# W1 staged in W2's tile and in the second `hT` buffer, with a new order of all operations

## The chip, the cores and the metric

The kernel runs on one core of one Trainium2 chip. The metric is the device time of one launch in microseconds; the time before is the median of three runs.

The core has five engines that run their own instruction streams: TensorE (PE in the profile; its weight loads are PEld), VectorE (DVE), ScalarE (ACT), GpSimd (POOL) and SyncE (SP), which here only issues DMAs. Loads of the first batch, of v and of W1 are issued by SP, casting loads (fp32 in memory, fp16 on chip) by POOL.

## The reference

Nystrom attention with 32 landmarks, in fp32, over 8 batches, 8 heads, 576 positions and 64 columns per head. Then, on the heads put side by side (`x` is 8 x 576 x 512), a normalisation, two products with a relu between them, and the residual.

```python
q_lm = q.reshape(B, H, 32, 18, D).mean(axis=3)
k_lm = k.reshape(B, H, 32, 18, D).mean(axis=3)
A, Bm, C = sm(q, k_lm), sm(q_lm, k_lm), sm(q_lm, k)     # softmax of scaled products
Z = Bm^T / (norm1(Bm) * norminf(Bm) + 1e-06)
for _ in range(6):
    Z = 2 * Z - Z @ Bm @ Z
x = heads_side_by_side(A @ Z @ C @ v)                   # 8 x 576 x 512
xn = (x - mean) / sqrt(var + 1e-06) * g_ln
out = x + maximum(xn @ w_ch1, 0) @ w_ch2                # 512 -> 2048 -> 512
```

## The kernel before

**Operations and their order.** Every piece of work is a named operation with the buffers that it uses and the engines that may do it. `op(name, engines, uses, fn)` only records it. At the end one loop goes through the list `ORDER`, 1571 entries of an operation's number and an engine's letter (P, D, A, G, S for PE, DVE, ACT, POOL, SP), and emits them. So that list sets the order of instructions on each engine, and which engine does what. A buffer takes a slot of its kind at its first use and gives it back behind its last use, so the list also decides who shares a slot with whom: kind `stg` has 6 slots (staged fp32 inputs), `p2` and `bank` are the PSUM kinds (2 and 4 slots), `nat` has 3, and `hT0` and `hT1` one each.

**Batch 0**, the first some 25 us, has a path of its own. SP loads its k, q and v as fp32 into `stg` slots, two units of four heads each (operations `load_k00`, `load_k01` and so on). They are cast to fp16, transposed by PE (`pst_k`, `pst_q`), summed to landmarks by PE (`pss_k`, `pss_q`), and copied out as `klm` and `qbd`. From these come the 32 x 32 softmax, six iteration steps (PE into `it`, DVE into `st`), the exponentials `ea` and `ect`, their normalisation through `psd` and `lns`, `product_0` (`pscv`, with v), `zt` and `zcbd`.

**The second half of each batch.** `psy` (operation `rows`) makes blocks of 128 rows of `x` from `ea` and `zcbd`. `psm` multiplies `zt` by a quarter of W1, and DVE or ACT makes `m` of it. For batches 0 and 1, `m` also takes up `less`, W1's column means, which PE makes in `psf` and ACT copies out, so that the mean of `x` is taken off. `psh` makes one of 16 hidden chunks (128 hidden columns, 576 positions) in one of the two `p2` slots. A relu on ACT (L203) or DVE (L1068) takes it into `hT`. `pso` multiplies `hT` by W2; batches 2 to 7 do that with seven products instead of eight for most blocks (`ps7a`, `ps7c`, `ps7e`), with sums (`mix`) made by POOL and DVE. The last block of all is cut into part a (384 columns) and part b (128 columns), each with its products, its closing addition on DVE (L210, `x<-pso_74a` and `x<-pso_74b`) and its stores.

**The weights.** `def_weights` loads W1 in 8 pieces of 128 x 2 x 512 fp32 by SP (`load_w1_0` to `load_w1_7`; piece i is half of hidden quarter i/2), each into a `stg` slot (`w1s`). 16 scalings multiply each half piece by g into the fp16 tile `w1_16` (two a piece, on POOL, DVE or ACT, which `ORDER` says). Four casting loads on POOL's queue bring W2 into `w2_16`. A W1 piece can only be loaded when one of the six `stg` slots is free, and these hold k, q and v of batch 0 first.

**Fillers.** `warm_0` is 24 idle matmuls of 160 columns into a `bank` slot; `warm_1` to `warm_14` are 4 idle matmuls of 128 columns each. They compute nothing that is used.

**Batch 1 and later** come from POOL's casting loads, `load_q10` the first of them, into `nat` slots, and are transposed by DVE (`xT_q<-nat_q`). Batch 1's landmark sums are made by PE (`psl`) and copied out as `tot`.

In the rows of the instruction lists below, `w_16_78` is W1's fp16 tile, `w_16_79` is W2's, `natv_76` and `natv_77` are v of batches 0 and 1, `w1s` a staged piece of W1.

Of the kernel before, what the change touches and what calls it, by code (L numbers as in the profile page):

```python
# [24 lines left out]
145P 169D 104A 168D 98S 254D 149P 150D 147P 148A 172P 173A 176P 247P 177A 248A 259D 255D 174P 175A
246D 256P 257A 146A 170P 171D 109G 110G 121P 122P 123P 111G 124P 268P 156P 258D 151D 249D 267P 112A
125A 275A 269A 270A 271A 157D 277A 158D 131P 132P 133P 134P 178P 163P 278D 279D 117G 273A 433G 274A
99S 113G 135A 180D 263S 164A 159P 280P 281D 160A 165P 166A 114G 264A 100S 115G 116G 265S 118G 136P
137P 266G 161P 179D 429G 119G 138P 139P 162D 282P 283D 140A 181P 182A 183P 284P 276D 285A 143P 187P
184D 286P 144A 188A 272D 152D 185P 186A 287D 297P 298D 299D 189P 191D 190D 288P 289A 294P 290P 295A  # L30
201P 202P 296A 300P 301A 291D 292P 293A 120G 455G 212P 213P 435G 436G 437G 310P 438G 445G 302A 303G
308P 309A 214P 330P 434D 444D 312D 311D 313D 332D 192P 193A 153D 154D 198P 199A 155A 441D 430D 439D
431D 331D 442D 440D 432D 443D 234P 556D 215P 304P 235P 236P 305A 306A 196P 446G 447G 203P 204P 194P
195A 237P 238P 205P 206P 451G 197A 307G 314P 315A 337P 339P 448G 449D 822G 338A 555D 239P 240P 241P
322P 207P 208P 574D 565D 569G 450D 340A 323A 216P 242D 209D 210S 217P 324D 341P 343D 223P 335P 244S
336A 342D 333P 463D 218P 219P 577G 452D 220D 344P 352P 353D 467G 468G 469G 470G 334A 826G 348P 345A
349A 346P 347A 457G 318P 319A 224P 316P 317A 225P 226P 227P 481P 458G 465D 459G 460G 482A 350P 454D
354D 357P 471D 464D 472D 351A 453D 363P 228P 229P 364D 358A 361P 230P 362A 461D 462D 365D 493P 494A
359P 368P 360A 483P 495P 355P 325D 326D 505A 369A 356A 231D 233A 200G 374P 375P 366P 367A 370P 371A
573G 506D 456D 507P 508P 509D 320P 321D 385P 484P 486A 487A 489A 510P 834D 511D 466D 491A 386P 387P  # L40
485A 388P 211S 512P 376P 473S 474G 490A 377P 496P 498A 501A 499A 497A 513D 514P 327D 488D 492D 328D
396P 397P 475S 476G 566G 828G 829G 830G 831G 572G 477S 478G 838G 839G 844G 564G 568G 503A 378P 379P
380P 515D 823D 502A 221S 504D 372P 516P 479S 480A 500D 517D 836D 528P 529P 530D 531D 398P 399P 373A
381P 522P 518P 389P 329A 866S 382D 418P 519D 824D 559D 520P 521D 523A 532P 419P 420P 524A 533A 534A
558D 550P 551D 552D 553D 548P 549A 421P 422P 423P 536P 424P 425P 848G 535G 832D 833D 554D 232S 867A
537A 538A 539G 560D 525P 527A 400P 401P 557D 426D 427S 605P 526A 606A 840G 841G 594P 595A 561D 540P
541A 390P 391P 611P 612A 837D 596D 827D 392P 393D 825D 850G 851G 852G 563D 603P 604A 853G 562D 859D
842D 860G 861G 843D 579P 613P 614A 407P 580A 601P 602A 609P 610A 1217G 585P 408P 845D 599P 409P 607P
600A 410P 411P 586A 597P 608A 542A 543G 856D 615P 598A 576G 626P 616A 412P 413P 581P 627A 402P 862G
394S 582A 570G 567D 617D 589D 835D 863G 858D 590D 618P 619A 634P 635A 643P 583P 584A 620P 621A 624P  # L50
414P 571G 874P 625A 622P 623A 628P 629A 644P 544P 847D 857D 545A 846D 591D 546A 875D 403P 632P 872S
633A 645P 630P 647P 592D 631A 646P 415D 877P 648P 649P 650P 864D 865D 854D 404D 855D 1191G 886P 638D
637G 641G 663P 664P 665P 639D 640D 662G 428S 417S 406S 661D 593A 882A 884A 879A 880A 883A 652D 878A
651D 657D 887A 889P 892A 896A 658D 666P 668D 894A 895A 849D 667D 653P 654P 711P 722P 712A 723A 891A
890A 655P 656P 547G 575G 675P 676P 677P 728P 729A 678P 695P 696A 1192D 713D 716P 881D 1194D 717A
724P 725A 876P 888P 1213G 660D 587P 870S 714P 416S 659D 871G 873G 384S 1229G 642G 1230G 1231G 726P
898A 715A 679D 682D 669P 897D 727A 588A 730P 222S 1232G 899D 900P 901P 731A 718P 732P 902D 743P 719D
578G 903P 904D 670P 720P 734A 733A 721D 744A 671P 672P 673D 699P 700A 893D 739P 636G 1203D 1239S
701P 905P 243S 741P 906D 740A 751P 674D 742A 703P 752A 907P 735P 736A 737P 383S 868S 681S 680S 683S
738A 702D 908D 909P 1219G 1195G 1220G 1221G 685P 704D 697P 698A 915P 917A 916A 910D 911P 1222G 759P  # L60
760P 749P 811P 925P 750A 761P 885D 869G 921P 926A 927A 753G 922P 1225D 755G 912D 913P 705D 706D 745P
746A 1227D 812P 707D 708D 709D 710A 813P 814P 747P 748A 686P 687P 688P 928G 929P 930A 1223D 1224D
1196D 1233D 815P 816P 923D 1228D 924D 914D 931A 1214D 943P 947D 944D 941P 817P 946D 945D 1240G 754G
# [12 lines left out]
1026D 1027D 1254D 1279D 1266D 1011G 1022P 1297G 1070P 1023P 1024P 1025P 1029D 1028D 1005G 1068P
1069D 1286A 1298P 1290P 1299A 1291P 1292D 1010D 1293D 1280P 1281D 1091P 1032P 1033P 1038P 1300A
1301G 1092A 1287P 1071D 1289A 1288A 1282P 1283D 1039P 1040P 1312P 1314D 1313D 1316D 1315D 1080P
1082A 796S 1099P 1100A 1081A 1034P 1035P 806S 1310P 1311A 1097P 1036D 1098A 1041P 1306P 1101P 1307A
1095P 1096A 1037D 1030D 1044P 1043D 1093P 1094A 1089P 1090A 1042D 1074D 1075D 1031G 807S 1045P 1046P  # L80
1083P 1084D 1047P 1103A 1051D 1317P 1318A 1087P 1088A 1102D 1085P 1086A 1054P 1052S 1055P 1106P
1107A 1104P 1048D 1049S 1105D 1319P 1320A 1056P 1057P 1061D 1076D 1108P 1058D 1109A 1110P 1111A
1122G 1126G 1124G 1180P 1181P 1112P 1113A 1063S 1343P 1332P 1344A 1182P 1183P 1114P 1115A 1128P
1129P 1120P 1121D 1118P 1119A 1130P 1131P 1053S 1116P 1117A 1077D 1078D 1351P 1352D 1079A 1308A
1309G 1123G 1125G 1137D 1062S 1136D 1184P 1185P 1349P 1350A 1186P 1187P 1302P 1138P 1334D 1333A
1337P 1303A 1132P 1133P 1338D 1188D 1134P 1347P 1348D 1341P 1342D 1135P 1143D 1142D 1148P 1050S
1190S 1327D 1149P 1150P 1304A 1323P 1151P 1153D 1324D 1152D 1345P 1346A 1339P 1340A 1139P 1140P
1141P 1335P 1353P 1147D 1144D 1145D 1354A 1364P 1336D 1355D 1146D 1127G 1154P 1155P 1365A 1325P
1326D 1156P 1189A 1360P 1361A 1356P 1357A 1157P 1370P 1160P 1161P 1372P 1305D 1433P 1162P 1435P
# [19 lines left out]
def kernel(  # L109
# [112 lines left out]
    def dma(e, o, i):  # L222
        keep(ENGINES[e].dma_start(out=o, in_=i))
# [1040 lines left out]
```

## Time and profile before

| | |
|---|---|
| time, median of 3 runs | 260.66 us (260.17 to 260.79) |
| span of the profiled execution | 258.5 us |
| PE busy | 249.9 us (97%) |
| PE weight loads | 179.8 us (70%) |
| DVE busy | 212.3 us (82%) |
| POOL busy | 177.5 us (69%) |
| ACT busy | 163.9 us (63%) |
| DMA, SP's queue | 23.37 MB, 29.6% of 16 engines' span |
| DMA, POOL's queue | 10.36 MB, 25.1% |
| granted TensorE clock | 0.9 or more in each of 40 slices |

One execution was profiled, and its own time is the span in the table, 258.5 us, from the first instruction to the last; the timed median lies 2.2 us above it. In the rows of the profile, L and a number is a line of the kernel before; `a<-b` says that a is written from b; sizes are partitions x columns. A row of the timeline begins with the start in us from the span's beginning and a duration, of one instruction or of a row of alike ones up to the end of the last; what stands in brackets is the idle time before it and who ended it. `SP` issues, `DMA` rows are transfers.

Read by slices, PE is busy nearly throughout, and its first slice is at seven tenths. The DMA engines move 234 to 374 GB/s in the first five of the 40 slices.

### The profile page before, as it was taken

How to read it: one execution, taken by the hardware profiler on the slowest of the kernel's cores; microseconds unless marked ns; L12 is line 12 of the kernel's file. 1: busy time of each engine (PE TensorE's matmuls, PEld its weight loads, DVE VectorE, ACT ScalarE, POOL GpSimd, SP SyncE). 2: the span in 40 equal slices, each digit the busy share in tenths (PEclk: the TensorE clock that was granted, in tenths of full speed). 3: DMA queues.
4: the chain of work that ended last, by engine and by line, in shares of the span. 5: the costliest groups of instructions: out<-in, count | busy, mean ns of one | idle time of the engine just before them, and what ended most of it. 6: DMA issues, size and time to landing. Idle time of an engine off the chain costs nothing.

```text
span 258.5 us, 8351 instructions
## 1 busy us (share of the span) xinstructions
PE 249.9 (97%) x3499; PEld 179.8 (70%) x3499; DVE 212.3 (82%) x472; ACT 163.9 (63%) x304; POOL 177.5 (69%) x180
## 2 busy tenths in 40 slices
PE   7898999999999999999999999999999999999993
PEld 7766465556554557777766787777867787788981
DVE  1669899999999989997998869898547999878661
ACT  1588886747766999778756997868666245644000
POOL 8324899689794789699999995782078505966600
PEclk9999999999999999999999999999999999999999
DMA  6999999999749176949704832500130100510356
GB/s 234 367 269 338 374 210 208 207 235 244 227 127 178 29 164 87 221 89 286 140 4 121 231 93 61 127 3 3 41 85 0 44 20 9 115 23 20 82 121 184
DMA packets 23277, 36.32 MB, mean 140 GB/s; under 512 B 2116, under 2 KB 11592, under 8 KB 23240
## 3 DMA queue, kind: packets, MB, share of 16 engines
q1 hardware_dynamic: 12456, 23.37, 29.6%
q0 software_dynamic: 9504, 10.36, 25.1%
q10 hardware_dynamic: 1280, 2.07, 3.1%
q8 instruction: 27, 0.44, 0.7%
q14 instruction: 10, 0.08, 0.1%
HBM read 36.70 MB, written 9.44 MB: 178 GB/s over the span
## 4 chain that ended last, share of the span: by engine, by line
PE 85%; DMA 7%; ACT 3%; DVE 2%; issue 1%; SPq 1%; ACTq 0%; DVEq 0%
PE psh L193 23%; PE ps7a L193 16%; PE pso L193 15%; PE ps7c L193 8%; DMA w1s<-in_moe_w_ch_dram 5%; PE ps7e L193 4%; PE psm L193 3%; PE psy L193 3%; DMA stg_q<-in_q_dram 3%; PE it L193 2%; PE pscv L193 2%; PE psd L193 1%; PE psec L193 1%; PE psea L193 1%; PE pso_74a L193 1%
## 5 line engine op out<-in xcount | busy, mean ns | idle before, releaser
L203 ACT ACTIVATE hT<-psh 128x576 f16<-128x576 f32 x106 | 65.8, 650 | 30.4 <-PE psh L193 28.6
L193 PEld LDWEIGHTS <-hT 128*128 128x128 f16 x688 | 64.6, 98 | 22.6 <-issue 3.1
L193 PE MATMUL psh<-ea,m 128*128 128x288 f16 x512 | 78.2, 286 | 0.1
L193 PEld LDWEIGHTS <-m 128*128 128x128 f16 x512 | 48.9, 98 | 15.6 <-issue 1.3
L193 PE MATMUL pso<-w,hT 128*128 128x512 f16 x176 | 45.5, 380 | 0.0
L207 POOL TENSOR_TENSOR mix<-hT 128x1024 f16<-128x1024 f16 x8 | 17.0, 2125 | 27.4 <-ACT hT L203 27.4
L210 DVE SCALAR_TENSOR_TENSOR x<-ps7a,rstd,x 128x256 f32<-128x256 f32 x48 | 21.3, 477 | 6.7 <-PE ps7a L193 4.9
L193 PE MATMUL ps7a<-mix,hT 128*128 128x256 f16 x192 | 25.9, 273 | 0.0
L1068 DVE TENSOR_SCALAR hT<-psh 128x576 f16<-128x576 f32 x22 | 16.4, 753 | 10.1 <-PE psh L193 9.9
L997 DVE BATCH_NORM_STATS2 six<-x 128x6 f32<-128x512 f32 x36 | 24.2, 673 | 0.0
L207 POOL TENSOR_TENSOR ea<-ea,lns 128x576 f16<-128x576 f16 (+1 forms) x14 | 17.7, 1261 | 7.2 <-ACT lns L203 4.0
L200 ACT CAST m<-psm 128x512 f16<-128x512 f32 (+1 forms) x25 | 19.1, 793 | 4.5 <-PE psm L193 3.4
L200 ACT COPY x<-psy 128x512 f32<-128x512 f32 (+1 forms) x29 | 16.8, 587 | 7.6 <-PE psy L193 7.2
L193 PEld LDWEIGHTS <-mix 128*128 128x128 f16 x192 | 18.2, 98 | 4.3 <-issue 1.5
L207 POOL TENSOR_TENSOR mix<-mix,hT 128x1024 f16<-128x1024 f16 x8 | 16.9, 2124 | 6.2 <-DVE mix L207 5.8
L207 POOL TENSOR_TENSOR hT<-hT 128x1024 f16<-128x1024 f16 x9 | 19.1, 2123 | 0.2
L207 POOL TENSOR_TENSOR hT<-hT,mix 128x1024 f16<-128x1024 f16 x7 | 15.1, 2166 | 4.4 <-PE ps7e L193 2.5
L214 DVE TENSOR_REDUCE part<-xT_k 128x32 f16<-128x576 f16 x24 | 17.1, 737 | 0.0
L207 POOL TENSOR_TENSOR asum_q<-asum_q 128x256 f32<-128x256 f32 (+1 forms) x24 | 15.1, 628 | 1.5
L203 ACT ACTIVATE ec<-psec 128x256 f16<-128x256 f32 (+1 forms) x42 | 12.4, 428 | 5.3 <-PE psec L193 5.3
L193 PE MATMUL psy<-zcbd,ea 128*128 128x256 f16 x80 | 14.8, 273 | 0.2 <-ACT x L200 0.2
L200 POOL CAST natv<-stg_v 128x1152 f16<-128x1152 f32 (+1 forms) x12 | 13.8, 1163 | 1.4 <-DMA stg_v<-in_v_dram 1.3
(174 smaller groups left out, 471.2 us busy)
## 6 DMA issues: line engine op xcount, KB each, us to landing
out_dram<-x SPq DMA_DIRECT2D x55, 128.0 KB, 2.7
stg_v<-in_v_dram SPq DMA_DIRECT2D x10, 576.0 KB, 5.1
w1s<-in_moe_w_ch_dram SPq DMA_DIRECT2D x8, 512.0 KB, 11.6
nat_q<-in_q_dram POOLq DMA_DIRECT2D x7, 576.0 KB, 8.7
nat_k<-in_k_dram POOLq DMA_DIRECT2D x7, 576.0 KB, 7.5
w<-in_moe_w_ch_dram POOLq DMA_DIRECT2D x4, 512.0 KB, 8.5
out_dram<-x ACTq DMA_DIRECT2D x15, 128.0 KB, 2.4
stg_v<-in_v_dram SPq DMA_DIRECT2D x6, 288.0 KB, 4.5
```

What stands on the lines that cost most here:

```text
L193: keep(nc.tensor.matmul(o, l, r, start=start, stop=stop, tile_position=(rb, cb), skip_group_check=(skip or cb != 0)))
L200: keep(nc.scalar.copy(o, i) if e == "A" else ENGINES[e].tensor_copy(out=o, in_=i))
L203: keep(nc.scalar.activation(*args, **kw))
L207: keep(ENGINES[e].tensor_tensor(out=o, in0=a, in1=b, op=f))
L210: keep(ENGINES[e].scalar_tensor_tensor(out=o, in0=a, scalar=s, in1=b, op0=f0, op1=f1))
L214: keep(nc.vector.tensor_reduce(out=o, in_=i, axis=axis, op=f))
L997: keep(nc.vector.bn_stats(out=T(f"six_{j}")[:], in_=T(f"x_{j}")[:]))
L1068: keep(nc.vector.tensor_scalar(out=o, in0=T(psh)[:, :, 0:HS], scalar1=0.0, scalar2=None, op0=ALU.max))
```

## The change

Two edits.

**1. Places of W1's pieces.** The eight pieces no longer go through `stg` slots. Pieces 0 to 3 are loaded into W2's tile (each takes the room of four of its 16 slices, read as fp32), and pieces 4 to 7 into the buffer of `hT_1`, the relus' output of batch 1, of which `held` makes the loads and the scalings of these pieces users. The scalings read from there. W2's loads stay casting loads on POOL's queue into the same tile, and so follow the scalings of the pieces in it.

```diff
     def def_weights():
+        if hT(1) not in kinds:
+            buf(hT(1), "hT1", [P, MCH, S + 64], FP16)
+
+        def place_of(i):
+            f, half = divmod(i, 2)
+            if f < 2:
+                return w2_16[:, ts(i, 4), :].rearrange("p m d -> p (m d)").bitcast(FP32).rearrange(
+                    "p (c d) -> p c d", c=2)
+            return T(hT(1))[:].rearrange("p m t -> p (m t)")[:, ts(i - 4, 4 * DM)].bitcast(FP32).rearrange(
+                "p (c d) -> p c d", c=2)
+
+        def held(i):
+            return () if i < 4 else (hT(1),)
+
         for i in range(8):
-            n = f"w1s_{i}"
-            buf(n, "stg", [P, 2, DM], FP32)
             f, half = divmod(i, 2)
-            op(f"load_w1_{i}", "S", (n,),
-               lambda e, n=n, f=f, half=half: dma(
-                   e, T(n)[:], w1_src[:, 2 * half:2 * half + 2, ts(f, DM)]))
+            op(f"load_w1_{i}", "S", held(i),
+               lambda e, i=i, f=f, half=half: dma(e, place_of(i), w1_src[:, 2 * half:2 * half + 2, ts(f, DM)]))
...
-                    o, src = w1_16[:, kk, ts(f, DM)], T(n)[:, c, :]
+                    o, src = w1_16[:, kk, ts(f, DM)], place_of(i)[:, c, :]
...
-                op(f"scale_w1_{i}{c}", "GAD", (n,), scale)
+                op(f"scale_w1_{i}{c}", "GAD", held(i), scale)
```

**2. The list `ORDER`** is another one throughout; the operations in it are the same. A line of it as it was and as it is:

```diff
 ORDER = """
-0G 20P 23P 4S 12P 14P 24P 17P 11P 2S 1S 3S 6S 7S 10P 21P 28G 38P 25A 26D 34P 39D 40P 29P 30A 31P 27D
+0G 23P 4S 11P 21P 20P 24P 28D 13P 18P 14P 19P 12P 15P 250G 22P 17P 2S 16P 26D 38P 40P 34P 42D 39A 1S
```

What moves in it, as far as the prediction speaks of it. In SP's queue, W1's pieces went 2, 3, 1, 0, 4, 5, 6, 7 and now go 2, 3, 0, 1, 4, 5, 6, 7, and `load_v01` goes ahead of `load_v00`. On PE, `warm_0` and eight other fillers stood at the program's head, ahead of the first transposes; now the other 14 stand there, and `warm_0` stands behind the transposes and sums of k. `product_0` stood between the second and the third iteration step and now stands behind the sixth. `rows_00` and `rows_01` now stand ahead of the product of `zt` and the second quarter of W1. Behind batch 1 the sums, blocks and chunks are interleaved in another way, a few of the sums change between POOL and DVE, and 25 relus between ACT and DVE (16 go to ACT, nine the other way). The program's last products and addition were part a's, behind part b's; now part b's come last.

Three places in rows. POOL's list ahead of its first loads, before and then of the change; the first row is the last of the constants, the next ones are casts of staged inputs, and `load_q10` and `load_k10` are the two DMA rows.

```order
L282 COPY spread_72<-ident_64 32x64
L200 CAST nat_k<-stg_k 128x2x9x64
L223 DMA nat_q<-in_q_dram 128x4x576
L223 DMA nat_k<-in_k_dram 128x4x576
L200 CAST natv_76<-stg_v 128x2x9x64
L357 TENSOR_SCALAR w_16_78<-w1s,g_sb 128x512 x2
L207 TENSOR_TENSOR ea<-ea,lns 128x288
```

```order
L282 COPY spread_72<-ident_64 32x64
L223 DMA nat_q<-in_q_dram 128x4x576
L200 CAST nat_q<-stg_q 128x2x9x64
L200 CAST natv_76<-stg_v 128x2x9x64
L223 DMA nat_k<-in_k_dram 128x4x576
L200 CAST natv_76<-stg_v 128x2x9x64
L207 TENSOR_TENSOR ea<-ea,lns 128x288
L367 TENSOR_SCALAR w_16_78<-w_16_79,g_sb 128x512
```

The cast of k goes to DVE, both casts of v and one of q come here, so `load_q10` follows the constants at once and `load_k10` stands between the two casts of v.

DVE's list from the last iteration step (`st<-st,it 128x2x32`) to the making of `m` for the first quarter of W1, before and then of the change:

```order
L210 SCALAR_TENSOR_TENSOR st<-st,it 128x2x32
L220 STREAM_TRANSPOSE xT_q<-nat_q 128x576
L200 CAST zt<-pszt 128x2x32
L214 TENSOR_REDUCE zsum<-pszc 128x2
L200 CAST zt<-pszt 128x2x32
L220 STREAM_TRANSPOSE lmt_q<-tot_q 128x64
L207 TENSOR_TENSOR zcbd<-pszc,heads_71 128x256 x2
L207 TENSOR_TENSOR ea<-ea,lns 128x288
L210 SCALAR_TENSOR_TENSOR m<-less,zsum,psm 128x512 x2
```

```order
L210 SCALAR_TENSOR_TENSOR st<-st,it 128x2x32
L643 TENSOR_SCALAR cv<-pscv,rcv,cinv 128x130 x2
L214 TENSOR_REDUCE zsum<-pszc 128x2
L367 TENSOR_SCALAR w_16_78<-w_16_79,g_sb 128x512
L207 TENSOR_TENSOR zcbd<-pszc,heads_71 128x256 x2
L207 TENSOR_TENSOR ea<-ea,lns 128x288
L200 CAST tot_q<-psl_q 128x128
L220 STREAM_TRANSPOSE xT_q<-nat_q 128x576
L210 SCALAR_TENSOR_TENSOR m<-less,zsum,psm 128x512 x2
```

A scaling of W1 stands ahead of `zcbd` now, the transpose of batch 1's q stands right ahead of `m`, and the two copies of `zt` have gone to ACT.

ACT's list from its first relus to the first copy of `less` behind batch 1's exponentials, before and then of the change:

```order
L203 ACTIVATE hT<-psh 128x576 x2
L200 CAST tot_k<-psl_k 128x128
L203 ACTIVATE hT<-psh 128x576
L200 CAST tot_k<-psl_k 128x128
L200 COPY x<-psy 128x512
L203 ACTIVATE w_16_78<-w1s,g_sb 128x512
L200 CAST less<-psf 128x512
L203 ACTIVATE ec<-psec 128x2x2x32
```

```order
L203 ACTIVATE w_16_78<-w_16_79,g_sb 128x512
L203 ACTIVATE hT<-psh 128x576 x2
L200 CAST less<-psf 128x512
L203 ACTIVATE hT<-psh 128x576
L200 CAST tot_k<-psl_k 128x128
L203 ACTIVATE hT<-psh 128x576
L200 CAST tot_k<-psl_k 128x128
L203 ACTIVATE w_16_78<-hT,g_sb 128x512
L203 ACTIVATE ec<-psec 128x4x2x32
```

A scaling now stands ahead of the first relu, `less` behind the second, and four relus of batch 0 stand here instead of three.

More of the change, by code (lines that the diff above doesn't have):

```diff
@@ L25 @@
[L25 to L39, printed above, removed]
@@ new lines @@
+1056P 1057P 1051D 1053S 1106P 1105A 1107A 1108P 1308A 1109D 1055P 1074D 1110P 1111A 1180P 1343P
+1332P 1112P 1181P 1309G 1182P 1183P 1344A 1349P 1058D 1113A 1350A 1061D 1116P 1184P 1117A 1118P
+1119A 1128P 1130P 1114P 1115D 1120P 1334A 1131P 1185P 1302P 1121A 1122G 1123G 1303A 1076D 1079A
+1129P 1333D 1137D 1347P 1348A 1335P 1336A 1132P 1134P 1136D 1186P 1059A 1341P 1342A 1135P 1323P
+1339P 1124D 1140P 1187P 1126G 1188D 1345P 1133P 1340A 1346A 1138P 1351P 1364P 1125G 1352D 1324A
+1146G 1353P 1355A 797A 1062S 1141P 1143D 1139P 1145D 1354A 1337P 1338D 1148P 1150P 1151P 1360P 1365A
@@ new lines @@
+1144D 1361A 1149P 1330D 1372P 1373D 1152D 1190A 1319P 1320D 1366P 1367A 1153D 1154P 1328D 1358P
+1359A 1142D 1327D 1127G 1155P 1356P 1147D 1357A 1304A 1368P 1156P 1370P 1369A 1371A 1305D 1052A
+1157P 1376G 1063A 1162P 1160P 1163P 1362P 1189S 1158D 1449P 1460P 1159D 1451A 1172P 1363D 1450A
+1161P 1164D 1381P 1461D 1170P 1171P 1441P 1442A 1173P 1174D 1382P 1375G 1177D 1179A 1321P 1464P
+1458P 1465A 1167D 1322D 1447D 1169A 1168A 1401P 1402P 1377G 1060A 1385P 1383P 1329D 1331A 1452P
+1386P 1459D 1435P 1380D 1384P 1389D 1453A 1175A 1403P 1390D 1462P 1387P 1454P 1436D 1463A 1439P
@@ new lines @@
+1374G 1466P 1378D 1440A 1393P 1394P 1446D 1455D 1437P 1438A 1388P 1395D 1467A 1391P 1392P 1396D
+1468P 1469A 1397D 1398D 1404P 1406D 1399G 1456P 1470P 1472A 1481P 1482A 1379G 1405D 1413P 1457A
+1407P 1409P 1471D 1410P 1433P 1489P 1400D 1414P 1444D 1490D 1477P 1478A 1178S 1325P 1326A 1408P
+1412D 1411D 1473P 1474A 1434A 1415P 1475P 1476A 1416P 1479P 1420D 1423P 1421A 1497P 1480D 1485P
+1486A 1501P 1424P 1491D 1493D 1503P 1487P 1417D 1488A 1418S 1483P 1445D 1443D 1484A 1492D 1494D
+1425P 1426P 1498P 1496D 1422S 1502P 1495G 1430D 1432S 1431S 1165A 1448A 1517P 1499P 1500P 1506D
@@ L105 @@
+1505D 1504P 1516D 1511D 1427D 1515D 1518P 1519P 1509P 1429S 1520P 1522D 1166A 1510P 1521D 1507P
+1508P 1514D 1176S 1549P 1428S 1550P 1419S 1513D 1512D 1529P 1531P 1523P 1525P 1526P 1524P 1528D
+1527D 1530P 1551P 1532P 1536D 1539P 1533D 1535A 1540P 1541P 1538S 1542P 1543D 1546D 1552P 1553P
+1537A 1534S 1548S 1554P 1555P 1556P 1545G 1560P 1561P 1562P 1563P 1564P 1565P 1547A 1544G 1557D
+1566P 1559A 1558S 1567P 1568D 1570A 1569S
 """
```

133 lines of the change are left out of this document (62 added, 71 removed).

## The prediction

> **What bounds the kernel now.** I read the busy times by stretch first, for where TensorE (PE) stands still: each row has a stretch, its length, the busy us of PE, its weight loads, DVE, ACT and POOL, then PE's granted clock and the DMA engines' share.
>
> ```profile
> 40.00:60.00 20.00, 20.00 (x161) 10.93 (x160) 19.79 (x40) 12.45 (x25) 16.50 (x21) 1.00 1.18 228
> 140.00:160.00 20.00, 19.90 (x280) 15.58 (x265) 16.55 (x37) 17.52 (x33) 18.45 (x16) 1.00 0.54 147
> ```
>
> From 40 us on PE is full, with one stretch at 19.90 of 20.00. It has the same matmuls before and after, so the change can win only in the first 40 us, at the seams between matmuls, and at the end. The chain of waits, windowed and whole, says what holds the start:
>
> ```profile
> 2.32 7.08 DMA stg_q<-in_q_dram
> ...
> 15.84 11.95 DMA w1s<-in_moe_w_ch_dram
> ...
> 254.19 0.62 DVE x L210
> ```
>
> A W1 transfer, 11.95 us under way, looks like the thing to mend. But was it late because it was issued late? The traffic by queue (packets, MB, share of the engines), from 11 to 18 us, and in the last row from 24 to 31; q1 is SP's queue, q0 POOL's:
>
> ```profile
> q0 software_dynamic: 604, 0.68, 57.8%
> q1 hardware_dynamic: 622, 1.22, 52.3%
> ...
> q1 hardware_dynamic: 1371, 2.74, 103.8%
> ```
>
> The 16 engines are full in both. SP alone moves 2.74 MB in 7 us, 0.39 MB/us; beside POOL's load it moves 1.22, 0.17 MB/us.
>
> **W1's new places.** Earlier issue brings no byte sooner where the engines are full: ahead of the last W1 piece stand the same k, q, v, W1 pieces and both loads of batch 1. What does move is POOL's first load, `load_q10`.
>
> ```profile
> 4.47 0.23 POOL L282 COPY spread<-ident 32x64 f16<-32x64 f16 x1
> 6.12 1.37 POOL L223 DMA_DIRECT2D nat_q<-in_q_dram  x1
> 19.75 0.69 POOL L357 TENSOR_SCALAR w<-w1s,g_sb 128x512 f16<-128x512 f32 x1 [1.51 <-DMA w1s<-in_moe_w_ch_dram]
> 32.08 1.36 POOL L357 TENSOR_SCALAR w<-w1s,g_sb 128x512 f16<-128x512 f32 x2 [0.62 <-DMA w1s<-in_moe_w_ch_dram]
> ```
>
> The cast of k goes to VectorE (DVE), so the load is issued at 4.47 + 0.23 = 4.70, 1.4 us sooner, and shares the engines 1.4 us sooner. SP loses 1.4 x (0.39 - 0.17) = 0.3 MB, which at 0.17 MB/us is **1.7 us for the second W1 piece**: 21.4 instead of 19.7 (the row at 19.75 waits for it). v, which now shares too, is later by as much, but its product is moved behind the iteration's last step. The last piece still lands at 32.0 (the row at 32.08). So the new places buy nothing by themselves, and sharing W2's tile and `hT1` costs nothing: the scalings that free them end near 33.5 (the two in the row at 32.08 are the last), W2's four loads stand behind them in POOL's queue as before, and batch 1's hidden chunks, which write `hT1`, stand behind batch 0's first output blocks on PE. If a scaling came late, W2's first load would, and PE has a dozen chunks in front of it.
>
> **The start.** PE, DVE:
>
> ```profile
> 1.40 6.26 PE L193 MATMUL idle<-zeros 128*128 128x128 f16 x56 [1.40 <-DVE zeros L252]
> 7.50 0.67 PE L197 MATMUL pst_k<-ident,nat_k 128*128 128x128 f16 x9
> 8.00 0.69 PE L193 MATMUL pss_k<-pm,nat_k 128*128 128x64 f16 x18
> 10.24 0.44 PE L193 MATMUL pss_q<-pm,nat_q 128*128 128x64 f16 x9 [0.18 <-DVE nat_q L200]
> 10.79 0.42 DVE L207 TENSOR_TENSOR qbd<-pss_q,mask 128x256 f16<-128x256 f32 x1 [0.41 <-PE pss_q L193]
> ```
>
> The 24 idle matmuls of 160 columns (`warm_0`) move behind the first transposes. By the rows, 9 x 128 columns take 0.50 us there (7.50 to 8.00), 0.43 ns a column, so they cost 24 x 160 x 0.43 = 1.65 us. k is transposed and summed by 8.7, the filler ends near 10.4, and the sums of q that started at 10.24 start there as a pair and end about 0.4 us later: `qbd` near 11.2. The six steps behind it lose three other DVE jobs from between them and win that back. I take 0, and 0 to +0.4 as bounds.
>
> **Up to the eighth hidden chunk.** What stood on DVE between the second piece and the first `psh`, and how PE went on:
>
> ```profile
> 20.84 0.72 DVE L207 TENSOR_TENSOR zcbd<-pszc,heads 128x256 f16<-128x256 f32 x2
> 21.48 0.44 DVE L207 TENSOR_TENSOR ea<-ea,lns 128x288 f16<-128x288 f16 x1
> 21.96 1.41 DVE L210 SCALAR_TENSOR_TENSOR m<-less,zsum,psm 128x512 f16<-128x512 f16 x2
> 24.17 0.76 DVE L220 STREAM_TRANSPOSE xT_q<-nat_q 128x576 uint32<-128x576 uint32 x1
> 23.48 1.14 PE L193 MATMUL psh<-ea,m 128*128 128x288 f16 x8
> ...
> 33.16 0.65 PE L193 MATMUL psh<-ea,m 128*128 128x288 f16 x4
> 33.65 0.59 PE L193 MATMUL psf<-w,lesser 128*128 128x512 f16 x2
> 34.25 1.14 PE L193 MATMUL psh<-ea,m 128*128 128x288 f16 x8
> ```
>
> Now DVE scales half of that piece itself, ahead of `zcbd`: 21.4 + about 0.6 = 22.0 (DVE's own scaling has no row; the fp32 cast of k, 1152 columns in 0.76, and POOL's 0.69 bound it at 0.3 and 0.7). Then 0.72 + 0.44 reach 23.2, where the rows that PE now takes ahead of `psm` can begin; the transpose (0.76), a small cast (0.25) and `m` (1.41) reach 25.6. **First psh at 25.6, not 23.48.**
>
> From there to the end of the eighth chunk PE has 8 `psh` at 0.49 (33.16 to 33.65), 10 `psf` at 0.215 (two of them and a step lie from 33.65 to 34.25), 18 `psl` at 0.055 like the transposes above, and some 1.6 of `psm`, `psec` and small ones: 8.6 us, so 34.2. But ScalarE (ACT) now takes the relus that DVE had among them:
>
> ```profile
> 19.92 0.72 ACT L203 ACTIVATE w<-w1s,g_sb 128x512 f16<-128x512 f32 x1
> 28.44 0.56 ACT L200 CAST less<-psf 128x512 f16<-128x512 f32 x1
> 28.91 1.08 ACT L203 ACTIVATE ec<-psec 128x128 f16<-128x128 f32 x4
> 29.99 0.79 ACT L203 ACTIVATE ec<-psec 128x256 f16<-128x256 f32 x2
> 31.54 1.19 ACT L203 ACTIVATE hT<-psh 128x576 f16<-128x576 f32 x2 [0.33 <-PE psh L193]
> ```
>
> Six relus before the one that frees the last chunk's buffer, at 1.19 / 2: 3.6; `less` twice 1.1; two scalings 1.4; `ec` 1.9; `tot` twice and a small `it`, each on a quarter or less of `less`'s columns, some 0.7. That is some 8.7 from the first chunk's end (25.6 + 0.65), 34.95, and with its 0.49 the eighth chunk ends at 35.4. The kernel before stood at this point at 34.25 (its ninth chunk starts there), 34.4 with the one `psy` group that the change has done more, less a step that it has not. **+1.0 us.** Bounds: the last W1 piece allows 32.0 + 0.7 + 0.43 + 0.2 + 0.49 = 33.9, so -0.5; with 8.6 us of PE and as much waiting as before had there (1.6), 36.3 with the start's 0.4, so +1.9.
>
> **Seams.** PE pays when it changes between whole matmuls and small tiles:
>
> ```profile
> 144.90 0.60 PE L193 MATMUL ps7c<-mix 128*128 128x256 f16 x4
> 145.43 0.41 PE L193 MATMUL psm<-w,zt 64*32 64x512 f16 x8
> 145.77 0.61 PE L193 MATMUL ps7a<-mix 128*128 128x256 f16 x4
> ```
>
> Four such `ps7c` need 4 x 0.109 = 0.44 in a run, here 0.53; `psm` needs 0.22 for 512 columns, here 0.34. About 0.1 a change. In the two lists I count 106 and 100 changes of tile shape behind `psh_001`: **-0.6 us**, bounds -0.9 (changes between whole and tiled alone, 98 and 88) and 0.
>
> **Tail.** The last block's quarter, not its three quarters, now ends the program: the closing addition takes 0.35 instead of 0.62.
>
> ```profile
> 252.57 0.35 DVE L210 SCALAR_TENSOR_TENSOR x<-pso_74b,rstd,x 128x128 f32<-128x128 f32 x1 [0.43 <-PE pso_74b L193]
> ```
>
> **-0.3 us**, bounds -0.3 and +0.2, as its stores follow closer on others. **Middle:** a new order can only add waits to a full PE: 0 to 0.8 (0.1, the gap of the stretch at 140, in each of eight stretches); I take +0.2.
>
> **Sum:** 1.0 - 0.6 - 0.3 + 0.2 = +0.3 on the span of 258.5, so 258.8. The timed median is 2.2 us above that span; I keep the 2.2: **261.0**.
>
> **Two rules weighed.** Between 7.5 and 10.8 us only SP's queue moved data, though POOL's load was issued from 6.12 to 7.49. So its data waited over 3 us, and I let them start as late after the new issue, near 9.5:
>
> ```profile
> q1 hardware_dynamic: 596, 1.30, 105.3%
> ```
>
> The Trainium skill, DMA: Bandwidth & Descriptors, section Latency and other measured facts, gives about 1 us to the first byte of a GpSimd DMA. By that the load would share from about 7 us, an estimate from that page; the row disagrees.
>
> At the head, 56 idle matmuls (7,936 columns) took 6.1 us, 0.77 ns a column, against 0.43 behind 7.5: half speed until then. If half speed lasts into the moved filler, it takes 3.0 instead of 1.65, and the sums of q wait 1.3 us more. No row here shows half speed later than 7.5. The Trainium skill, TensorE: Matmul & The Clock Gate, section What's actually happening, has a free-running window of 3.4 us, so by it the end of half speed may fall elsewhere in another run.
>
> **Rivals.**
> - *The load's data start no sooner* (they waited for SP's transfers, not for the issue). For: the 3 us of silence above. Then the second piece lands at 19.7, the first `psh` is at 24.6, PE's count ends under the bound of 33.9, and ACT, with relus overlapped as well as its best rows, at 34.2: -0.2 - 0.6 - 0.3 = -1.1, **259.6**. Chance 0.27.
> - *Slower: ACT becomes the bound and waits too.* In its queue the two scalings of the first piece stand ahead of `lns`, and a scaling of the fourth ahead of the first relu; each that meets a piece not landed stops the relus behind it, and with two `p2` buffers PE stops as well. It decides once the pieces land over 0.5 us later than ACT reaches them. Then +1.9 + 0.4 (middle) - 0.6 - 0.0 = +1.7: **262.4**. Against: the same pieces now are waited for with other work at hand. Chance 0.20.
> - *Half speed in the filler*: +1.3 at the start, of which the second piece's landing hides all but 0.5: **261.5**, 0.05. *POOL's data start with the issue*, near 7: q's last piece, due at 9.4 (2.32 + 7.08), loses 2.4 x 0.22 MB and is 1.4 later, nothing hides it: **262.4**, 0.03, as the silence above speaks against it.
> - That the W1 move does not bring W1 sooner is in the forecast already.
>
> **Numbers.** Forecast 0.45, own range 260.3 to 261.7. A measurement tells 0.3%, 0.8 us, from no change. Faster: 0.24 of the first rival and 0.02 of the forecast. Slower: the second rival 0.20, the small ones 0.06, the forecast's upper end 0.04. Same: the rest, 0.44. Range 259.4 to 262.5, from just under the first rival to just over the second.
>
> **What would show it.** The first `psh` at 25 to 26, the second W1 piece's scaling at 21 to 22, the last at 32; ACT without a gap from 26 to 35; PE full from 36; the sum of idle behind 40 under 1 us; the closing addition at 0.35. It is wrong if POOL's load lands no sooner than 18, if the first `psh` comes before 24, or if PE waits behind 40.

## The result and the profile after

The changed kernel takes 271.43 us (median of 4 runs, 268.72 to 272.82) where the kernel before takes 260.42. One of the four was in the slow state; ratios, here and below, are of fast runs alone, and this one is 1.0392, 95% interval 1.0339 to 1.0445. By it the change is **10.2 us slower**, far outside the range of the prediction (259.4 to 262.5), and 8 us above its slowest rivals (262.4).

The first page says where to look. Here are the busy time of the engines, the time by slices for PE and its granted clock, and the engines' shares of the chain of waits:

```profile
span 270.3 us, 8332 instructions
PE 253.1 (94%) x3499; PEld 179.9 (67%) x3499; DVE 215.2 (80%) x467; ACT 168.2 (62%) x318; POOL 162.8 (60%) x173
PE   7889998997999999983999999999999999999992
PEclk9999999998899999996899999999999999999999
PE 53%; DMA 25%; POOL 11%; DVE 3%; SPq 3%; issue 2%; ACT 0%; POOLq 0%; ACTq 0%
```

PE was full behind 40 us before. Now one slice of 6.8 us near 125 us is at three tenths, one near 63 us at seven, and the clock falls behind both. PE's share of the chain is 53% where it was 85%. The list of what PE waited for (total, times, longest) names three new waits; the idle matmuls at the head are as before:

```profile
PE ps7a L193 <- DVE x L210: 5.4, 1, 5.4
PE psh L193 <- ACT hT L203: 2.0, 1, 2.0
PE idle L193 <- DVE zeros L252: 1.4, 1, 1.4
PE pso L193 <- DMA w<-in_moe_w_ch_dram: 1.0, 2, 0.7
```

Busy time by stretch around the two gaps (length, busy us of PE, weight loads, DVE, ACT, POOL, then PE's clock, DMA share, GB/s):

```profile
64.00:66.00 2.00, 0.21 (x2) 0.18 (x2) 2.00 (x5) 1.97 (x3) 1.97 (x3) 0.99 0.16 15
66.00:69.00 3.00, 3.00 (x12) 1.53 (x11) 2.07 (x5) 2.42 (x5) 0.35 (x1) 0.50 1.02 165
...
120.00:126.00 6.00, 0.60 (x6) 0.34 (x5) 6.00 (x4) 1.19 (x2) 5.84 (x6) 0.83 0.98 177
126.00:132.00 6.00, 6.00 (x72) 3.65 (x71) 3.53 (x11) 2.34 (x4) 4.49 (x7) 0.60 0.25 81
```

In this execution each gap is paid twice. PE stands for 2.0 and 5.4 us, and then runs at 0.50 for 3 us and at 0.60 for 6 us, which by these rows is another 1.5 and 2.4 us. In the second gap DVE is busy for all of 6.00 us with four instructions. Its timeline there (start, duration), and POOL's beside it:

```profile
118.21 0.71 DVE L214 TENSOR_REDUCE part<-xT_k 128x32 f16<-128x576 f16 x1
118.84 6.30 DVE L207 TENSOR_TENSOR mix<-w,mix 128x512 f16<-128x512 f16 x1
125.06 0.86 DVE L210 SCALAR_TENSOR_TENSOR x<-ps7a,rstd,x 128x256 f32<-128x256 f32 x2
```

```profile
118.63 0.76 POOL L223 DMA_DIRECT2D nat_k<-in_k_dram  x1
119.42 2.13 POOL L207 TENSOR_TENSOR hT<-hT 128x1024 f16<-128x1024 f16 x1
121.50 1.15 POOL L207 TENSOR_TENSOR mix<-w 128x512 f16<-128x512 f16 x1
122.60 1.15 POOL L200 CAST natv<-stg_v 128x1152 f16<-128x1152 f32 x1
123.72 1.14 POOL L207 TENSOR_TENSOR asum_q<-nat_q 128x512 f32<-128x512 f16 x1
124.93 1.32 POOL L207 TENSOR_TENSOR asum_q<-asum_q 128x256 f32<-128x256 f32 x2
```

A DVE sum of 128 x 512 takes **6.30 us**. Grouped by shape, DVE's sums of this form show that it is one of three, with a median of 0.417:

```profile
L207 DVE TENSOR_TENSOR mix<-w,mix x3: 378/417/6302, 90.2 to 118.8; 128x512 f16<-128x512 f16 x3
```

That operation is `mix_36`, a piece of the W2 sums for the seven products; the old list gave it to POOL, the new one to DVE. It began at 118.84 and ended at 125.14, 0.28 us behind the end of POOL's `asum_q700` (124.86), and until then POOL's operations follow one another without a pause. The additions behind it on DVE (`x<-ps7a`) empty the PSUM buffer that PE waits for. The gap near 63 has another shape. On ACT, `cast_v31` waits for its load, and PE's chunks wait for the relus queued behind it:

```profile
64.03 1.17 ACT L200 CAST natv<-stg_v 128x1152 f16<-128x1152 f32 x1 [2.38 <-DMA stg_v<-in_v_dram]
65.10 1.18 ACT L203 ACTIVATE hT<-psh 128x576 f16<-128x576 f32 x2
```

In the old list that cast stood at 74.55 us, behind its load by 1.3 us.

### The profile page after: what moved, and what is told of

It is laid out like the page before. It is cut to its first block, busy times and chain, and to the rows that moved or that the text cites. A ratio compares the mean times of both kernels' runs of the same rounds, so it can differ in the third digit from the quotient of the medians.

```text
span 270.3 us, 8332 instructions
## 1 busy us (share of the span) xinstructions
PE 253.1 (94%) x3499; PEld 179.9 (67%) x3499; DVE 215.2 (80%) x467; ACT 168.2 (62%) x318; POOL 162.8 (60%) x173
## 4 chain that ended last, share of the span: by engine, by line
PE 53%; DMA 25%; POOL 11%; DVE 3%; SPq 3%; issue 2%; ACT 0%; POOLq 0%; ACTq 0%
PE ps7a L193 15%; PE psh L193 14%; DMA stg_v<-in_v_dram 12%; PE ps7c L193 7%; DMA hT<-in_moe_w_ch_dram 5%; DMA nat_k<-in_k_dram 4%; POOL asum_q L207 4%; PE pso L193 3%; PE ps7e L193 3%; DMA w<-in_moe_w_ch_dram 3%; SPq L223 3%; POOL mix L207 2%; DVE mix L207 2%; DMA nat_q<-in_q_dram 2%; PE psy L193 2%
## 5 line engine op out<-in xcount | busy, mean ns | idle before, releaser
L203 ACT ACTIVATE hT<-psh 128x576 f16<-128x576 f32 x113 | 70.4, 653 | 27.0 <-PE psh L193 25.2
L193 PE MATMUL psh<-ea,m 128*128 128x288 f16 x512 | 81.4, 293 | 2.0 <-ACT hT L203 2.0
L193 PEld LDWEIGHTS <-m 128*128 128x128 f16 x512 | 50.1, 100 | 20.1 <-issue 4.3
L207 POOL TENSOR_TENSOR ea<-ea,lns 128x576 f16<-128x576 f16 (+1 forms) x14 | 17.2, 1227 | 29.4 <-DVE hT L1078 11.9
L200 ACT COPY x<-psy 128x512 f32<-128x512 f32 (+1 forms) x33 | 19.4, 590 | 16.1 <-PE psy L193 15.7
L207 POOL TENSOR_TENSOR mix<-hT 128x1024 f16<-128x1024 f16 x7 | 15.1, 2162 | 17.7 <-ACT hT L203 17.7
L200 POOL CAST natv<-stg_v 128x1152 f16<-128x1152 f32 (+1 forms) x13 | 16.1, 1241 | 13.2 <-DMA stg_v<-in_v_dram 10.1
L207 POOL TENSOR_TENSOR hT<-hT 128x1024 f16<-128x1024 f16 x7 | 15.8, 2263 | 9.1 <-DVE mix L207 8.9
L1078 DVE TENSOR_SCALAR hT<-psh 128x576 f16<-128x576 f32 x15 | 11.3, 754 | 9.7 <-PE psh L193 9.6
L207 POOL TENSOR_TENSOR hT<-hT,mix 128x1024 f16<-128x1024 f16 x5 | 11.8, 2356 | 5.1 <-PE ps7e L193 3.5
L207 POOL TENSOR_TENSOR asum_q<-nat_q 128x512 f32<-128x512 f16 x12 | 14.4, 1197 | 0.7 <-DMA nat_q<-in_q_dram 0.4
```

The source lines that it names most:

```text
L193: keep(nc.tensor.matmul(o, l, r, start=start, stop=stop, tile_position=(rb, cb), skip_group_check=(skip or cb != 0)))
L200: keep(nc.scalar.copy(o, i) if e == "A" else ENGINES[e].tensor_copy(out=o, in_=i))
L203: keep(nc.scalar.activation(*args, **kw))
L207: keep(ENGINES[e].tensor_tensor(out=o, in0=a, in1=b, op=f))
L1078: keep(nc.vector.tensor_scalar(out=o, in0=T(psh)[:, :, 0:HS], scalar1=0.0, scalar2=None, op0=ALU.max))
```

## The experiments

**The theory**: the order costs the loss, not W1's places, and nearly all of it in three waits: `mix_36` on DVE, `cast_v31` on ACT, and W2's second load behind `load_q20` in POOL's queue. The rivals: the places hold up something; or the waits only hide others, so that taking one away lets the next through. The entries of `ORDER` are numbers and letters; the text says which operation each is.

**1. The places alone.** The new `def_weights` with the old list.

```diff
 def def_weights():
+    if hT(1) not in kinds:
+        buf(hT(1), "hT1", [P, MCH, S + 64], FP16)
...
 ORDER = """
 0G 20P 23P 4S 12P 14P 24P 17P 11P 2S 1S 3S 6S 7S 10P 21P 28G 38P 25A 26D 34P 39D 40P 29P 30A 31P 27D
```

> The new places of W1 with the old order. Theory (the order, not the places, costs the 11 us): 260.4 us, within 0.8 of the kernel before, no gap on PE over 1 us behind 40 us. Rival (the places hold up W2 or the hidden chunks): 262 us or more, with a PE wait for W2 between 36 and 52 us.

Measured: 260.59 us against 260.35, ratio 1.0016 (0.9998 to 1.0034), and no gap over 0.2 us behind 40 us. Within the 0.3% of that interval the places cost nothing and bring nothing. The first scalings began at 17.31 us, and the last at 32.91, as before (17.56 and 32.74).

**2. `mix_36` back on POOL** (its number is 578).

```diff
-730P 1205D 578D 888P 876P
+730P 1205D 578G 888P 876P
```

> The changed kernel with one operation, mix_36 (the sum of 128x512 that took 6.30 us on DVE at 118.8), put back on POOL at the same place of the order. Theory (this one blocked operation costs its gap of 5.4 us on PE and the clock behind it): 7 us less than the changed kernel, 264.4, and no PE gap over 1 us near 120. Rival (the gap only hides another wait, of PE for batch 3's loads or for POOL): 268 or more, with a gap of over 2 us within 10 us behind that place.

Measured: 263.11 us, ratio 1.0091 (1.0056 to 1.0125). By the ratios that is 7.8 us less than the changed kernel, for 7 expected. The stretches there are full and at full clock:

```profile
116.00:122.00 6.00, 6.00 (x97) 4.84 (x94) 5.53 (x13) 4.95 (x12) 5.96 (x6) 1.00 1.04 158
122.00:128.00 6.00, 6.00 (x116) 4.02 (x101) 5.14 (x14) 4.97 (x8) 5.77 (x8) 1.00 0.83 186
```

One letter of the list holds three quarters of the loss.

**3. `cast_v31` later on ACT** (480), behind `x_14` (323).

```diff
-319A 369A 480A 226P 227P
+319A 369A 226P 227P
...
-229P 822G 323A 359P
+229P 822G 323A 480A 359P
```

> The changed kernel with cast_v31 (the cast on ACT that waited 2.4 us for its load at 61.7 to 64.0) moved behind two relus, a copy of lm and a copy of x on ACT. Theory (that cast at the head of ACT's queue makes PE's gap of 2.0 us at 63.4, and the lower clock behind it): 2.8 us less than the changed kernel, 268.6. Rival (the relus would wait for POOL or DVE work anyway): 270.5 or more.

Measured: 270.36 us, ratio 1.0381 (1.0347 to 1.0415). Beside the changed kernel's 1.0392 that is 0.3 us less, inside either interval, and not 2.8: no gain shows. The cast no longer waits for its load, but it still takes 1.19 us ahead of two relus, and PE waits 0.8 for them:

```profile
64.38 1.19 ACT L200 CAST natv<-stg_v 128x1152 f16<-128x1152 f32 x1
65.44 1.21 ACT L203 ACTIVATE hT<-psh 128x576 f16<-128x576 f32 x2
```

So this place was half right: the wait for the load is gone, and the length of the cast takes a part of its room. Nor was the gap of 2.0 us a fixed loss. In the six other traces whose lists are the same up to there (experiments 2 and 5) PE waits 0.4 to 1.9 us at that place, and runs at full clock behind it in all six. The 2.8 was priced from one execution.

**4. All three waits taken out**: the edits of 2 and 3, and `load_w2_1` (118) ahead of `load_q20`, behind `load_w2_0` (117).

```diff
-153D 263S 117G 258D 156P
+153D 263S 117G 118G 258D 156P
...
-184A 190D 118G 212P 285D
+184A 190D 212P 285D
```

> The changed kernel with its three long waits taken out together: mix_36 on POOL, cast_v31 behind the copy of x on ACT, and load_w2_1 right behind load_w2_0 in POOL's queue, ahead of load_q20. Theory (these three places are all that the new order loses, and its start gains nothing): 263.1 of the run with mix_36 alone, less 0.6 for the cast and 1.2 for W2, so 261.3. Rival (each wait removed lets the next one through): 262.5 or more. A version better than the kernel before would have to come under 259.9.

Measured: 262.89 us, ratio 1.0093 (1.006 to 1.0127): the rival's side. 7.8 us of the 10.2 are gone, and 2.4 stay. Experiment 2 alone won as much (1.0091), so the two other waits, taken out with it, bring nothing that shows in the time. Where the rest stays, the stretches tell; first this kernel, then the kernel before:

```profile
0.00:40.00 40.00, 35.59 (x585) 25.89 (x586) 27.90 (x75) 25.89 (x50) 25.83 (x53) 1.00 1.03 290
40.00:60.00 20.00, 19.77 (x196) 10.16 (x194) 18.46 (x35) 11.80 (x23) 16.63 (x19) 1.00 1.13 198
60.00:70.00 10.00, 9.18 (x120) 5.97 (x119) 9.93 (x20) 8.05 (x14) 6.92 (x10) 1.00 0.72 159
70.00:100.00 30.00, 29.45 (x490) 15.49 (x490) 27.74 (x60) 21.13 (x43) 22.97 (x25) 1.00 0.65 147
```

```profile
0.00:40.00 40.00, 35.88 (x615) 26.37 (x616) 28.91 (x81) 26.87 (x50) 24.98 (x54) 1.00 1.04 296
...
60.00:70.00 10.00, 10.00 (x161) 6.28 (x160) 9.32 (x24) 6.46 (x13) 8.48 (x10) 1.00 0.92 225
70.00:100.00 30.00, 30.00 (x472) 16.71 (x471) 28.35 (x57) 24.44 (x48) 23.53 (x28) 1.00 0.63 126
```

PE stands 0.29 longer up to 40 us, 0.23 from 40 to 60 (where it was full, 20.00), 0.82 from 60 to 70 and 0.55 from 70 to 100. That is 1.9, and with 0.4 at the program's end 2.3 of the 2.4 by which the two spans (260.9 and 258.5) differ.

**5. Why `mix_36` takes so long.** POOL's operations beside it were moved, with `mix_36` left on DVE, and then `mix_36` itself. First, the DMA issue in which it began (`load_k70`, 1213) behind `asum_q700` (1219):

```diff
-903P 732P 1213G 733A
+903P 732P 733A
...
-739P 736A 1219G 908D
+739P 736A 1219G 1213G 908D
```

> The changed kernel with one DMA issue of POOL, load_k70, moved from just ahead of hmix_224 to behind asum_q700; mix_36 stays on DVE, and POOL has four sums, casts and copies behind one another beside it. Theory 1 (DVE's sum gets no turn while POOL's operations follow each other without a gap): mix_36 takes 4 us or more again, 270 to 272. Theory 2 (it waits for the one POOL operation that runs when it comes, as DVE's long sums of the kernel before did): up to 2.1 us on top of its 0.4, 267 to 268. Theory 3 (it is the DMA issue on POOL, in which it began, that holds it up): 0.4 to 1 us, about 264.5.

Measured: 270.58 us, ratio 1.0384 (1.0361 to 1.0407), and `mix_36` took 6.68. So the DMA issue is not the cause, and it is not one running operation either: it sat through five (a copy, two sums, a cast and the first `asum` step).

Then the same DMA issue put inside that row of operations, between `mix_26` (574) and `cast_v40`:

```diff
-903P 732P 1213G 733A
+903P 732P 733A
...
-642G 734D 574G 672P
+642G 734D 574G 1213G 672P
```

> The changed kernel with load_k70 on POOL moved two operations on, from ahead of hmix_224 to between mix_26 and cast_v40; mix_36 stays on DVE. Theory 1 (DVE's sum gets its turn at POOL's first pause between sums, casts and copies, and a DMA issue is such a pause): mix_36 ends about 0.3 us behind mix_26 and takes some 4 us instead of 6.3. Theory 2 (it was the end of asum_q700 that let it through in all three traces): it ends 0.3 us behind asum_q700 again, 6 us or more.

Measured: 267.68 us in one run, PE's gap 2.9, and `mix_36` at 3.96. POOL's timeline and `mix_36`'s row of that kernel:

```profile
117.44 2.12 POOL L207 TENSOR_TENSOR hT<-hT 128x1024 f16<-128x1024 f16 x1
119.52 1.14 POOL L207 TENSOR_TENSOR mix<-w 128x512 f16<-128x512 f16 x1
120.61 0.77 POOL L223 DMA_DIRECT2D nat_k<-in_k_dram  x1
121.38 1.18 POOL L200 CAST natv<-stg_v 128x1152 f16<-128x1152 f32 x1
```

```profile
117.49 3.96 DVE L207 TENSOR_TENSOR mix<-w,mix 128x512 f16<-128x512 f16 x1
```

It ended at 121.45, just as that DMA issue ended (121.38), and 2.2 us ahead of the end of `asum_q700` (123.67). So the order of POOL's row sets when the sum ends, and theory 2 (that it needs the end of `asum_q700`) falls. Theory 1 (that any pause of POOL lets it through, a DMA issue too) stands only in part. The sum let go 0.8 behind `mix_26`, not 0.3. And in the changed kernel itself it came in a DMA issue (118.63 to 119.39) with 0.55 us of it left, more than the 0.38 that such a sum needs, and was not let through.

Does it matter in what it arrives? In the next three kernels POOL's copy `tail_2` (636) was moved behind `asum_q703`, `mix_36` two places later, and `mix_36` four places later.

```diff
-715A 726P 636G 727A 903P
+715A 726P 727A 903P
...
-873G 915P 1222G 909P
+873G 915P 1222G 636G 909P
```

> The changed kernel with tail_2, POOL's copy ahead of load_k70, moved behind asum_q703, so that POOL is about 1 us earlier and mix_36 comes in the middle of hmix_224 (a sum of two tiles), not in a DMA issue or a copy. Theory 1 (a pause of POOL lets it through): still 3.5 us or more, to the end of asum_q700. Theory 3 (what counts is what it comes in on: behind a running sum it is next, as center_30 and hmix_630 of the kernel before were): it ends 0.3 us behind hmix_224, 2.5 us at most.

Measured: 270.34 us in one run; `mix_36` took 6.49 and again ended 0.3 behind `asum_q700`. It had arrived in the DMA issue, with 0.73 us of it left, not in the sum, so this run told theories 1 and 3 apart only in part.

```diff
-730P 1205D 578D 888P 876P
+730P 1205D 888P 876P
...
-676P 725A 659D 720P
+676P 725A 659D 578D 720P
```

> The changed kernel with mix_36 two places later on DVE, behind the two additions add7_221 and add7_220 that PE waited for. The gap of 5.4 us on PE should go in any case, and the time fall to 264 to 266. Theory 1: mix_36 itself comes in hmix_224 and lasts to the end of asum_q700, 4 us or more. Theory 3: it ends 0.3 us behind hmix_224, under 2.5 us.

Measured: 269.52 us in one run. The gap of `ps7a` went, but another of 3.4 us came in its place, for the softmax behind `mix_36`. It took 5.57 and ended at 123.73, 0.28 behind `cast_v40`, and `asum_q700` took 1.33 there instead of 1.14, so this time it got in between the two, which follow each other without a pause. Again it had come ahead of `hmix_224`, and a whole DMA issue passed without letting it in:

```profile
118.16 5.57 DVE L207 TENSOR_TENSOR mix<-w,mix 128x512 f16<-128x512 f16 x1
```

```profile
118.33 0.76 POOL L223 DMA_DIRECT2D nat_k<-in_k_dram  x1
```

```diff
-730P 1205D 578D 888P 876P
+730P 1205D 888P 876P
...
-716P 682D 679D 717A
+716P 682D 679D 578D 717A
```

> The changed kernel with mix_36 four places later on DVE, behind add7_250, so that it comes while POOL's hmix_224 is under way (in all runs so far it came up to 2 us ahead of hmix_224's start, in a copy or a DMA issue). Theory 3 (a sum that comes while a POOL sum runs is next when that ends): 2.3 us at most, and no gap of PE over 1 us near 120. Theory 1 (it waits for a pause of POOL, wherever it comes): it ends with cast_v40 or asum_q700 again, some 3 us or more.

Measured: 269.19 us in one run. This time it came in the middle of the sum, which decides about theory 3:

```profile
118.93 4.70 DVE L207 TENSOR_TENSOR mix<-w,mix 128x512 f16<-128x512 f16 x1
```

```profile
117.89 2.14 POOL L207 TENSOR_TENSOR hT<-hT 128x1024 f16<-128x1024 f16 x1
119.98 1.15 POOL L207 TENSOR_TENSOR mix<-w 128x512 f16<-128x512 f16 x1
121.08 1.16 POOL L200 CAST natv<-stg_v 128x1152 f16<-128x1152 f32 x1
122.20 1.14 POOL L207 TENSOR_TENSOR asum_q<-nat_q 128x512 f32<-128x512 f16 x1
123.42 1.33 POOL L207 TENSOR_TENSOR asum_q<-asum_q 128x256 f32<-128x256 f32 x2
```

It waited through the running sum and three more, and ended at 123.63, behind `asum_q700` (123.34). The next `asum` step needs that one's output, and there POOL paused, by the profile for 0.08 us. Theory 3 falls. Theory 1 keeps this run, and has the one before against it, in which no pause let the sum in. What the seven traces with the long sum share is less: it sat through two to five of POOL's operations on tiles, and ended 0.3 us behind the last of them, once 0.8 us behind it at the end of a DMA issue.

**6. The move to DVE where POOL pauses.** In the kernel before, `mix_36` alone to DVE.

```diff
-743P 719D 578G 903P 904D
+743P 719D 578D 903P 904D
```

> The kernel before with mix_36 alone given to DVE, at its old place of the order, where POOL's operations beside it wait for one another (each asum step for the one ahead of it). Theory (the move to DVE costs only where POOL's operations follow each other with no pause): mix_36 lasts 0.4 to 1.6 us, PE has no gap over 1 us behind 100, and the time is 260.4, within 0.8. Rival (mix_36 is slow on DVE wherever POOL is busy): 4 us or more, and 263 or more.

Measured: 260.34 us against 260.51, ratio 0.9994 (0.9984 to 1.0004). `mix_36` took 0.69, beside `asum` steps that wait for one another:

```profile
120.16 0.69 DVE L207 TENSOR_TENSOR mix<-w,mix 128x512 f16<-128x512 f16 x1
```

```profile
119.31 1.25 POOL L207 TENSOR_TENSOR asum_q<-asum_q 128x256 f32<-128x256 f32 x2
120.64 0.49 POOL L207 TENSOR_TENSOR s_q<-asum_q,nat_q 128x128 f16<-128x128 f32 x1
```

It got through at 120.56, when the `asum` pair ended. The same letter costs 7.8 us in one list and nothing in the other.

**7. The two ends put back** in the kernel of experiment 4: `cast_k01` (28) on POOL ahead of `load_q10`, and the last block's part b ahead of part a (of that, the list's last entries are shown: 1557 and 1568 are the additions of parts a and b).

```diff
-20P 24P 28D 13P 18P
+20P 24P 28G 13P 18P
...
-1564P 1565P 1547A 1544G 1557D 1566P 1559A 1558S 1567P 1568D 1570A 1569S
+1569S 1549P 1550P 1551P 1547A 1544G 1552P 1553P 1554P 1555P 1556P 1557D 1559A 1558S
```

> The kernel with the three long waits taken out (262.89 us), and two ends put back: cast_k01 on POOL ahead of load_q10, so that this load is issued some 1.4 us later again, and the last block's part b ahead of part a. Theory (W1's second piece comes late because the load shares the engines sooner; and the program's end costs 0.4 more with part b last): that piece lands at 19.7 where it landed at 18.6 to 21.0, the first psh comes at 24.5, the span ends 4.4 us behind PE instead of 4.8, and the time is 261.6 to 262.2. Rival (the landing hangs on SP's queue, not on that load): the piece lands anywhere from 18.6 to 21.0 again and only the end's 0.4 comes back: 262.5.

Measured: 263.69 us, ratio 1.0124 (1.0107 to 1.0141), not faster than the 262.89 (1.0093) that it starts from. Most of its parts did what was said. `load_q10` was issued at 6.07 and landed at 18.69 instead of 17.19, W1's second piece landed at 19.8 instead of 21.0, and the span ended 4.1 us behind PE instead of 4.8. But the first `psh` came at 25.7, not at 24.5, and PE now waited for that load itself, since the new list has the landmark sums of batch 1's q early:

```profile
PE psl_q L193 <- DMA nat_q<-in_q_dram: 1.4, 1, 1.4
```

So in this order the early issue, which the forecast priced as a loss, saves PE that wait. That the wait is what ate up the gain is argued from this trace, not shown: two things were changed at once. None of these versions beats the kernel before.

## Why the prediction was wrong

**The step that failed** is one sentence: "a new order can only add waits to a full PE: 0 to 0.8 (0.1, the gap of the stretch at 140, in each of eight stretches)". It measured some 9: 7.8 for `mix_36` alone, and 1.6 of smaller waits behind 40 us that are left in experiment 4. Of the signs that the prediction named, "if PE waits behind 40" came true, with 8.4 us in three waits. The bound came from the gaps that PE had under the *old* list. These tell how well the old list covered its waits, not how long the waits are that another list can uncover. Waits of the kind stood in the trace of before, on the engines behind PE. Grouped by shape (least, median and longest ns), DVE's sums of two SBUF tiles read there:

```profile
L207 DVE TENSOR_TENSOR w<-w,less x8: 654/684/1541, 50.0 to 90.8; 128x1024 f16<-128x1024 f16 x8
L207 DVE TENSOR_TENSOR hT<-hT,mix x5: 679/682/1624, 107.5 to 223.4; 128x1024 f16<-128x1024 f16 x5
```

In both, the longest is more than twice the median, and each of these two ended some 0.55 us behind the end of a POOL operation: the same wait, met once for each and covered by other work. The forecast priced none of the sums behind batch 1 that changed engines, and looked at none of these maxima. They were a warning, not a price: both are 0.9 us above their median, and `mix_36` lost 5.9. The rest of what `mix_36` cost is PE's clock, at half behind the gap; the forecast had half speed only for the head.

**W1's places: right.** With the old list they bring nothing and cost nothing (experiment 1).

**The start: too dear.** The forecast gave +1.0 at the eighth chunk, which was to end at 35.4; it began at 33.3 and its next followed at 33.8, so in this execution the change stood 0.4 ahead of the 34.25 of before. In the eight other traces with the same head the next chunk began from 34.1 to 35.9, with a median of 34.8, which is 0.6 behind. So there was a loss, and it was smaller. `qbd` came at 11.14 for a forecast of 11.2. `load_q10` was issued at 4.66 and landed 1.1 us sooner (17.2 for 18.3), as foreseen. The term that was too large is the 1.7 us for W1's second piece: forecast at 21.4, it landed at 19.56 (19.67 before). In the eight other kernels with the new list and the early load it landed between 18.6 and 21.0, on average 0.5 later than before: it seems that the share of the engines that SP lost was over-counted. The first `psh` came at 24.5, and in other executions up to 26.6, around the 25.6 of the forecast. ACT's 8.7 us from there were about right (25.2 to 33.8).

**Seams: not seen.** With the waits taken out (experiment 4), PE is busy 250.1 us where it was 249.9, so the 0.6 for fewer changes of tile shape do not show.

**The tail: wrong sign.** Forecast -0.3; the span ends 4.7 to 4.85 us behind PE's last product in all nine kernels with part b last, instead of 4.35. The closing addition is at 0.35 as foreseen, but the last two stores are issued 0.6 us behind part a's, take 1.1 us to issue instead of 0.5, and land 3.2 us later instead of 2.4.

**The rivals.** The first (no gain from the load) and the third (half speed in the moved filler) did not occur. But in three of the nine traces with the new list and the early load the granted clock fell to 0.5 later in the head, between 15 and 27 us (experiments 2 and 5), and in none of the three with the old list; what that costs was not taken apart. The slower one, ACT as the bound, has the mechanism of the gap at 63 us (an ACT operation that waits for a transfer stops the relus behind it), but in another place and with v, not W1, and it was priced for the first 36 us only.

**What stays open.** The runs show that POOL's row holds `mix_36` up and sets when it ends, not what place in that row lets it through. A DMA issue did so in one order and not in others. In the kernel before, the DVE sum of 1.54 us got through behind one POOL operation whose successor had nothing to wait for, where `mix_36` sat through two to five. And it is one sum: of the 35 other sums that DVE writes into `mix`, `hT` and `w` in the changed kernel none took over 1.05 us. The 2.3 us of small waits in experiment 4 were located, not mended.

## What to carry to other kernels

When a list of orders changes throughout, don't bound its waits by the idle time of the busiest engine under the old list: look in the old trace at the longest duration of each kind of operation, not its mean, and ask for each what it met. That tells which waits there can be, not how long they get. An operation that changes engines is priced with its new neighbours. In these runs a DVE sum of two SBUF tiles was quick where POOL's operations depend on one another (0.69 us) and could be slow beside a row of independent ones; it should not stand there ahead of what frees a buffer that PE waits for. And a gap seen in one execution is not yet a fixed loss: the one near 63 us was 0.4 to 2.0 us from trace to trace.

## What the runs showed of the hardware

A DVE sum of two SBUF tiles (0.38 us at best) took 4.0 to 6.7 us beside POOL operations that followed one another, in seven kernels. The Trainium skill, SBUF — State Buffer, sections SBUF: two separate sides and Who interferes with whom, says that such a sum contends with GpSimd's reads of SBUF, and that whichever comes second waits until the first has finished. The contention agrees with these traces. The length does not: in the last run of experiment 5 the sum came in one POOL operation and sat through four, so there the page's rule was only a lower bound.

PE's clock fell to 0.50 behind each gap of 2.9 to 5.4 us, in seven traces. Of the shorter gaps near 65 us one did so, of 2.0 us, for 3 us; two of 1.9 us in experiment 5 were followed by full clock. In experiment 2 the clock was at half from 16 to 22 us with no gap over 0.4 us in the 5 us ahead of it. The Trainium skill, TensorE: Matmul & The Clock Gate, section What's actually happening, lets half rate follow an idle window of some 3.4 us. The gaps of 4.0 us and more agree; the falls behind 2.0 and 2.9 us, and the one at 16 us, came without an idle window of that length.

The landing of one and the same transfer, W1's second piece, was spread over 2.4 us (18.6 to 21.0) between nine executions whose queues held the same loads up to there.
